# A banded attention and a gated feed-forward block on one core: the head of batch 0, the order of the loads and the last output tile are rewritten

## The chip, the core and the metric

The kernel runs on one core of a Trainium2 chip. The core has five engines with a queue of instructions each: TensorE (PE in the profile; its weight loads stand apart as PEld), VectorE (DVE), ScalarE (ACT), GpSimd (POOL) and SyncE (SP). Instructions of one engine run in the order in which they are written, and wait for other engines through semaphores. Transfers are issued from SP's, ACT's or GpSimd's queue. The metric is the device time of one execution in microseconds (us), lower is better. Before the change it is 253.46 us, the median of 9 runs (252.95 to 253.99).

## What is computed

There are four batches of 768 tokens with 8 heads of 64. Each token attends to the first 8 tokens and to the last 96, with a bias that falls with the distance; the result, with the heads side by side, goes through a gated feed-forward block.

```python
scores = q @ k.T / sqrt(64) - slope[h] * dist      # kept where key < 8 or 0 <= q - key < 96
a = exp(scores - max); a = a / (sum(a) + 1e-9)
x = (a @ v).transpose(0, 2, 1, 3).reshape(3072, 512)
g = x @ w_gate
out = (g / (1 + exp(-g)) * (x @ w_val)) @ w_out     # w_gate, w_val 512 x 1536, w_out 1536 x 512
```

Inputs and output are float32; the kernel computes with fp16 operands and float32 accumulation.

## The kernel before

**Tiles.** Heads go in four pairs (`hp` 0 to 3), two pairs make a quad (`g` 0, 1). Keys go in seven chunks of 120 (the last has 48), each with the 8 global keys in front, so that a chunk fills 128 rows: `kTs` holds the transposed keys in this form, `vSs[b]` the values. The first 8 rows of `vSs` are copied there by SP from `vG` (`copy_globals`). Queries of a batch are cut in two halves of 384 tokens, and a half is one token tile `t` of the feed-forward block (eight in all).

**Attention of a pair.** q and k are transposed on TensorE (L296, L270) or, for later pairs, by DMA (L399); scores go to a PSUM bank (L343, L366), ScalarE takes the exponential (L351, L375) into `at`, and a mask multiply puts the bias in (L355, L383, L386). In the first half of batch 0 there is no mask multiply: the bias is added by a matmul of `slopeI` and `dist` in front of the scores (L332). Values and denominators of a quad are matmuls with `vS` and with ones (L443); VectorE transposes and inverts the denominator (L453, L454, L459), and x is the product of the two (L499, L478).

**Feed-forward.** For a tile `t` and each of 12 blocks `f` of 128 columns: the gate's four matmuls and the value's four (L516), a tanh on ScalarE (L527), two multiplies on VectorE (L529, L533) into `hT`. Each 128-token row of the output is 12 matmuls with `wo` (L545), issued in four parts of three, one evacuation (L559) and one store by SP. Only the very last output row is evacuated in halves by ScalarE and VectorE, out of one bank, and stored by ACT's and SP's queues (L554 to L557).

**The head** is everything before the first product, for the first half of batch 0. q and k of pairs 0 and 1 come as float32 through SP and are cast by ScalarE and VectorE (`p_cast`, L589); those of pairs 2 and 3 are cast by the DMA, issued from GpSimd. V comes as one transfer of 384 KB (`v16`) in the row order that makes long packets, and TensorE brings it into chunks with twelve matmuls against permutation matrices (`p_perm`, L598), which VectorE builds; chunk 3 is cut at token 384 and has a tile of its own (`vCut`). `fill` issues matmuls on ones, with no use but to keep TensorE busy.

**Order.** It is written by hand. After the head, `stretches` pairs a run of feed-forward blocks with a list of attention steps; a step is put in whenever a quota has been earned by the blocks. Work on ScalarE and VectorE that may come later waits in the list `later`, of which one entry is taken with each group. `half1` is the second half of batch 0, `first(1)` the first half of batch 1, `both(b)` the second half of `b` and the first of `b + 1`. Loads are tied to blocks by `at_step`. GpSimd has no more than eight of its transfers under way: each issue waits for the one eight before it.

```python
stretches = [
    (ff(0, 0, 10), half1),
    (ff(0, 10, 12) + ff(1, 0, 3), []),
    (ff(1, 3, 12, (1, 1, 2)), fst),
    (ff(2, 0, 12, (1,)) + ff(3, 0, 12, (1,)), both(1)),
```

GpSimd's loads stand in this order: V, then k and q of pairs 2 and 3, `vG`, the weights of `f` 0 to 3 (`load_w(0, ·)`, four transfers of 256 KB), the second half of k and q of batch 0 (384 KB each), the weights of `f` 4 to 7 (`load_w(1, ·)`), the rest of V, the weights of `f` 8 to 11, `wo`, and batch 1.

Of the kernel before, what the change touches and what calls it, by code (L numbers as in the profile page):

```python
# [9 lines left out]
FP32 = mybir.dt.float32  # L10
# [6 lines left out]
WIN = 216  # L17
# [20 lines left out]
def kernel(  # L38
# [32 lines left out]
        np.concatenate([np.eye(128, 160, dtype=np.float16), dist_np], axis=1), name="consts")  # L71
# [25 lines left out]
    consts = sb.tile([128, 160 + 3 * WIN], FP16, name="consts")  # L97
    nc.sync.dma_start(out=consts, in_=const_dr.ap())
    identx, ident, dist = consts[:, 0:160], consts[:, 0:128], consts[:, 160:]
# [3 lines left out]
    q32 = sb2.tile([128, H // 2, J2 * D], FP32, name="q32", tag="qst")  # L103
    k32 = sb2.tile([128, H // 2, J2 * D], FP32, name="k32", tag="kst")
    q16 = sb2.tile([128, 2, H, J2 * D], FP16, name="q16", tag="qst")
    k16 = sb2.tile([128, 2, H, J2 * D], FP16, name="k16", tag="kst")
    v16 = sb.tile([128, H, J2 * D], FP16, name="v16")
    for hp in range(2):
        for st, src in ((k32, k), (q32, q)):
            nc.sync.dma_start(  # L110
                out=st[:, 2 * hp:2 * hp + 2, :],
                in_=src[0, 2 * hp:2 * hp + 2, 0:TB, :].rearrange(
                    "h (p j) d -> p h (j d)", p=128))

    def load_half(dst, src, half, h0, h1):
        nc.gpsimd.dma_start(
            out=dst, in_=src[0, h0:h1, TB * half:TB * half + TB, :].rearrange(
                "h (p j) d -> p h (j d)", p=128))

    vSs = [sb.tile([128, NCH, H, D], FP16, name=f"vS{b}") for b in range(B)]  # L120
    for b in range(1, B):
        nc.gpsimd.memset(vSs[b][:, 6, :, :], 0.0)
    load_half(v16, v, 0, 0, H)
    load_half(k16[:, 0, 4:8], k, 0, 4, 8)
    load_half(q16[:, 0, 4:8], q, 0, 4, 8)

# [4 lines left out]
    NC0 = 4  # L131
    perm = sb.tile([128, J2, NC0, 128], FP16, name="perm")
    nc.vector.memset(perm.rearrange("p j c m -> p (j c m)").bitcast(mybir.dt.uint32), 0)
    kTs = [sb.tile([128, NCH * 128], FP16, name=f"kT{i}") for i in range(NP)]

    vS3 = sb.tile([128, H, D], FP16, name="vCut")


    nc.vector.memset(vSs[0][:, 6, :, :], 0.0)
# [3 lines left out]
    for j in range(J2):  # L143
        nc.vector.tensor_copy(
            out=perm[:, j, :, NG + j::J2],
            in_=identx.rearrange("p (c m) -> p c m", c=NC0))
        n = (NG - j + J2 - 1) // J2
        nc.vector.tensor_copy(
            out=perm[:, j, :, j:NG:J2],
            in_=identx[:, 0:n].unsqueeze(1).broadcast_to([128, NC0, n]))  # L150

# [31 lines left out]
    def copy_globals(b):  # L183
        c0 = 3 if b == 0 else 0
        nc.sync.dma_start(
            out=vSs[b][0:NG, c0:, :, :],
            in_=vG[:, b, :, :].unsqueeze(1).broadcast_to([NG, NCH - c0, H, D]))
# [71 lines left out]
    class Pair:  # L259
# [30 lines left out]
        def transposes_half(self, half, tr, k_eng):  # L290
            hp = self.hp
            trq, trk = tr
            for st, dst in ((k16, trk), (q16, trq)):
                for j in range(J2):
                    for hi in range(2):
                        nc.tensor.transpose(  # L296
                            dst[64 * hi:64 * hi + 64, 128 * j:128 * j + 128],
                            st[:, half, 2 * hp + hi, D * j:D * j + D], ident)
# [28 lines left out]
        def bias(self, half, which):  # L327

            sc = banks("sc")
# [86 lines left out]
    class Quad:  # L416
# [19 lines left out]
        def weigh(self, half, dst, side):  # L436
            b, g = self.b, self.g
            parts = self.parts(half)
            for i, (c, cb, col, o, n) in enumerate(parts):
                vals = vS3 if (b, half, c) == (0, 0, 3) else vSs[b][:, c]  # L440
# [96 lines left out]
    def out_part(t, i, part):  # L537
# [10 lines left out]
        if part == 3:  # L548
            osb = sb2.tile([128, DM], FP32, name="osb", tag="osb")
            r0 = TB * t + 128 * i  # L550
            if t == NT - 1 and i == 2:

                oB = sb2.tile([128, DM // 2], FP32, name="osb", tag="th")
                nc.scalar.mul(out=osb[:, 0:DM // 2], in_=ops[:, 0:DM // 2], mul=0.5)  # L554
                nc.vector.tensor_scalar_mul(oB, ops[:, DM // 2:], 0.5)
                nc.scalar.dma_start(out=out[r0:r0 + 128, 0:DM // 2], in_=osb[:, 0:DM // 2])
                nc.sync.dma_start(out=out[r0:r0 + 128, DM // 2:], in_=oB)  # L557
            else:
                nc.scalar.mul(out=osb, in_=ops, mul=0.5)  # L559
                nc.sync.dma_start(out=out[r0:r0 + 128, :], in_=osb)  # L560

# [4 lines left out]
    load_globals()  # L566
    copy_globals(0)
# [9 lines left out]
    rings = {"t": ["x0", "x1"], "v": ["x2", "o0"]}  # L577

    def p_single(name, ring, dt=FP32):
        tags = rings[ring]  # L580
        tags.append(tags.pop(0))
        return single(name, tags[-1], dt)

    def p_bias(hp):
        pairs[0, hp].scs = [pairs[0, hp].bias(0, 0), pairs[0, hp].bias(0, 1)]

    def p_cast(hp, k_eng, q_eng):
        for eng, dst, src in ((k_eng, k16, k32), (q_eng, q16, q32)):
            eng(out=dst[:, 0, 2 * hp:2 * hp + 2], in_=src[:, 2 * hp:2 * hp + 2])  # L589

    def p_tr(hp, k_eng):
        tr = [p_single("trs", "t", FP16) for _ in range(2)]
        pairs[0, hp].transposes_half(0, [t[:, 0:TB] for t in tr], k_eng)

    def p_perm(c, eng):
        psv = p_single("psv", "v")
        for j in range(J2):
            nc.tensor.matmul(  # L598
# [237 lines left out]
```

The softmax here doesn't subtract the row's maximum and nothing guards it: scores larger than these inputs give would overflow.

## Time and profile before

| | |
|---|---|
| median of 9 runs | 253.46 us (252.95 to 253.99) |
| the profiled execution | 253.44 us, of which the span (first to last instruction) is 251.7 |
| granted TensorE clock | 0.998 |
| PE busy | 239.6 us (95%), 2384 matmuls |
| DVE busy | 166.9 us (66%) |
| ACT busy | 131.0 us (52%) |
| POOL busy | 106.2 us (42%), its DMA issues among it |
| GpSimd's DMA queue | 65408 packets, 13.83 MB, 67.4% of the 16 engines' span |
| one group of four matmuls, 128x384 | 0.65 us from start to start |

The page cuts the span into 40 slices of 6.29 us and gives the busy share of each in tenths. A timeline row is: start, duration (us), engine, line, operation, output and inputs, count, and in brackets how long the engine was idle before it and what ended that. The chain of work that ended last is given as start, duration, engine and line. A matmul's duration has its latency in it, so rows of TensorE overlap.

### The profile page before, as it was taken

The numbers are of one execution on the slowest core, as the hardware profiler recorded it, in microseconds if no ns is written. First come the engines' busy times: TensorE is split into PE (matmuls) and PEld (weight loads), VectorE is DVE, ScalarE is ACT, GpSimd is POOL, SyncE is SP. The second block draws the span as 40 slices with busy tenths as digits, with TensorE's granted clock in tenths as the row PEclk, the third lists the DMA queues.
The fourth block names the chain that finished last, engine by engine and source line by source line (L and its number), as shares of the span: only waits on it lengthen the run. The fifth ranks groups of instructions, "written<-read, shape, count | busy, mean of one in ns | idle before, by whom it ended". The sixth has DMA issues, their size and how long they took to land.

```text
span 251.7 us, 5999 instructions
## 1 busy us (share of the span) xinstructions
PE 239.6 (95%) x2384; PEld 135.3 (54%) x2384; DVE 166.9 (66%) x379; ACT 131.0 (52%) x290; POOL 106.2 (42%) x123
## 2 busy tenths in 40 slices
PE   7888999899889999999999999999999999999994
PEld 4564556464445555555555556555555555555541
DVE  6356779856785675979775656978766666556510
ACT  3475787559464565454753644555725634332221
POOL 9753674460056966904509776803030242200000
PEclk9999999999999999999999999999999999999999
DMA  6999999992850999996917998991011101100122
GB/s 160 176 205 179 180 203 207 173 134 52 126 69 8 160 131 110 188 139 110 81 44 83 147 154 97 144 101 43 0 44 42 44 0 44 43 26 19 42 83 83
DMA packets 86499, 25.63 MB, mean 102 GB/s; under 512 B 76288, under 2 KB 83528, under 8 KB 86472
## 3 DMA queue, kind: packets, MB, share of 16 engines
q0 software_dynamic: 65408, 13.83, 67.4%
q1 hardware_dynamic: 20920, 11.30, 22.4%
q8 instruction: 18, 0.29, 0.5%
q10 hardware_dynamic: 144, 0.13, 0.2%
q14 instruction: 9, 0.07, 0.1%
HBM read 28.63 MB, written 6.29 MB: 139 GB/s over the span
## 4 chain that ended last, share of the span: by engine, by line
PE 81%; DVE 8%; ACT 4%; DMA 3%; issue 1%; POOL 1%; DVEq 0%; ACTq 0%; POOLq 0%
PE ops L545 23%; PE gps L516 23%; PE vps L516 22%; DMA v<-in_v_dram 3%; PE sc L366 3%; PE num L443 3%; PE den L443 2%; DVE sl L529 2%; ACT at L351 2%; ACT th L527 1%; PE psv L598 1%; DVE hT L533 1%; PE trs L296 1%; PE sc L343 1%; DVE dT L453 1%
## 5 line engine op out<-in xcount | busy, mean ns | idle before, releaser
L529 DVE SCALAR_TENSOR_TENSOR sl<-th,gps 128x384 f32<-128x384 f32 x94 | 51.8, 551 | 45.4 <-ACT th L527 44.4
L527 ACT ACTIVATE th<-gps 128x384 f32<-128x384 f32 x94 | 46.5, 494 | 63.1 <-PE gps L516 61.6
L516 PE MATMUL gps<-xT,wg 128*128 128x384 f16 x376 | 77.0, 326 | 0.7 <-DVE xT L478 0.6
L516 PE MATMUL vps<-xT,wv 128*128 128x384 f16 x376 | 76.5, 326 | 0.5 <-DVE sl L529 0.4
L545 PE MATMUL ops<-wo,hT 128*128 128x512 f16 x288 | 75.5, 379 | 0.0
L533 DVE TENSOR_TENSOR hT<-vps,sl 128x384 f16<-128x384 f32 x94 | 51.7, 551 | 7.2
L478 POOL TENSOR_TENSOR xT<-ns,rb 128x384 f16<-128x384 f32 x24 | 24.2, 1028 | 75.4 <-DVE rb L459 61.3
L516 PEld LDWEIGHTS <-wg 128*128 128x128 f16 x384 | 35.8, 98 | 33.1 <-issue 3.1
L516 PEld LDWEIGHTS <-wv 128*128 128x128 f16 x384 | 36.8, 98 | 26.4 <-issue 2.1
L545 PEld LDWEIGHTS <-hT 128*128 128x128 f16 x288 | 27.4, 98 | 25.1 <-issue 0.4
L375 ACT ACTIVATE at<-sc 128x432 f16<-128x432 f32 x72 | 33.6, 535 | 9.0 <-PE sc L366 9.0
L171 POOL DMA_DIRECT2D vS<-in_v_dram x25 | 22.3, 898 | 9.6 <-DMA wg<-in_moe_w_gate_dram 2.5
L559 ACT ACTIVATE osb<-ops 128x512 f32<-128x512 f32 x23 | 13.7, 597 | 18.0 <-PE ops L545 18.0
L474 ACT COPY ns<-num 128x384 f32<-128x384 f32 x28 | 12.0, 482 | 12.0 <-PE num L443 11.2
L203 POOL DMA_DIRECT2D qst<-in_q_dram x20 | 16.8, 857 | 2.7 <-DMA wo<-in_moe_w_out_dram 1.6
L203 POOL DMA_DIRECT2D kst<-in_k_dram x20 | 17.0, 867 | 2.1 <-DMA wo<-in_moe_w_out_dram 1.0
L386 DVE TENSOR_TENSOR at<-at,masks 128x864 f16<-128x864 f16 x20 | 12.1, 605 | 4.6 <-ACT at L375 4.6
L351 ACT ACTIVATE at<-sc 128x432 f16<-128x432 f32 (+2 forms) x32 | 11.5, 447 | 3.9 <-PE sc L343 3.9
L386 POOL TENSOR_TENSOR at<-at,masks 128x864 f16<-128x864 f16 x4 | 7.3, 1822 | 13.6 <-ACT at L375 13.6
L443 PE MATMUL num<-at,vS 128*32 128x216 f16 (+6 forms) x560 | 12.0, 226 | 0.0
L443 PE MATMUL den<-at,ones 128*32 128x216 f16 (+6 forms) x288 | 9.2, 229 | 1.9 <-DVE at L383 1.4
L453 DVE STREAM_TRANSPOSE dT<-den 128x384 f32<-128x384 f32 x16 | 9.2, 576 | 1.8 <-PE den L443 1.7
(76 smaller groups left out, 169.9 us busy)
## 6 DMA issues: line engine op xcount, KB each, us to landing
out_dram<-osb SPq DMA_DIRECT2D x23, 256.0 KB, 2.0
vS<-in_v_dram POOLq DMA_DIRECT2D x21, 120.0 KB, 9.2
kst<-in_k_dram POOLq DMA_DIRECT2D x20, 96.0 KB, 5.1
qst<-in_q_dram POOLq DMA_DIRECT2D x20, 96.0 KB, 5.1
wg<-in_moe_w_gate_dram POOLq DMA_DIRECT2D x6, 256.0 KB, 9.0
wv<-in_moe_w_val_dram POOLq DMA_DIRECT2D x6, 256.0 KB, 9.5
wo<-in_moe_w_out_dram POOLq DMA_DIRECT2D x3, 512.0 KB, 11.0
k<-in_k_dram SPq DMA_DIRECT2D x2, 192.0 KB, 3.6
```

What stands on the lines that cost most here:

```text
L171: nc.gpsimd.dma_start(out=vSs[b][NG:NG + n, c, :, :], in_=v[b, :, KC * c:KC * c + n, :].rearrange("h p d -> p h d"))
L203: nc.gpsimd.dma_start(out=rows_of(st, b, h // 2)[:, :, h % 2, :], in_=src[b, h].rearrange("(t p) d -> p t d", p=128))
L351: nc.scalar.activation(out=at[:, hi, 0:col + n], in_=sc[hi][:, 0:col + n], func=AF.Exp, scale=scale)
L375: nc.scalar.activation(out=at[:, hi, :], in_=sc[hi][:, 0:BANK], func=AF.Exp, scale=scale)
L386: mul_eng.tensor_mul(at, at, m[:, :, o:o + BANK])
L443: nc.tensor.matmul(dst[r, o:o + n], lhsT=ones[:, 0:32] if side is None else vals[:, 4 * g + j, side::2], rhs=pairs[b, 2 * g + j // 2].at[c ...
L478: mul_eng.tensor_mul(self.x_out(half, side), srcs[side], self.rb)
L516: nc.tensor.matmul(gv[f, which][:, 0:TB], lhsT=w[:, c, 128 * f:128 * f + 128], rhs=x_of(t)[:, c, :], start=(c == 0), stop=(c == NC - 1))
L527: nc.scalar.activation(out=th, in_=dst[:, 0:TB], func=AF.Tanh, scale=0.5)
L529: nc.vector.scalar_tensor_tensor(out=sl, in0=th, scalar=1.0, in1=dst[:, 0:TB], op0=AluOp.add, op1=AluOp.mult)
L533: nc.vector.tensor_mul(hTs[t][:, f, :], dst[:, 0:TB], gv["sl"])
L545: nc.tensor.matmul(ops, lhsT=hTs[t][:, f, 128 * i:128 * i + 128], rhs=wo[:, f, :], start=(f == 0), stop=(f == NFF - 1))
```

## The change

- **Head.** One pair's q and k (pair 0) come as float32, k through SP and q through ACT's queue; pairs 1 to 3 are cast by the DMA, from GpSimd. V of batch 0 comes in chunks as for the other batches, with no permutation matmuls and no `vCut`; the four chunks of the first half stand ahead of the weights on GpSimd. The constants are split into `ident` (SP) and `dist` (ACT's queue). The memsets of `vSs` go from GpSimd to VectorE. Scores of a pair are two units of two banks, placed by name over the eight banks, and units of different pairs interleave with transposes.
- **Loads.** All of GpSimd's loads up to the end of batch 1 stand in one row after the first transposes. The weights of `f` 4 to 7 come ahead of the second half of k and q of batch 0.
- **Order.** The first five blocks have no attention steps, the ten steps of `half1` go into `f` 5 to 9. In `first(1)` the scores of pair 2 come ahead of the values of quad 0, and the DMA transposes of pairs 2 and 3 one step earlier. In `both` one spreading of keys goes one step earlier.
- **Last output row.** Two banks of 256 columns, 12 matmuls each; the first is evacuated by VectorE and stored by SP, the second by ScalarE and stored by its own queue.

```diff
-    identx, ident, dist = consts[:, 0:160], consts[:, 0:128], consts[:, 160:]
+    nc.sync.dma_start(out=ident, in_=const_dr.ap()[:, 0:128])
...
+    nc.sync.dma_start(out=k32, in_=half_of(k, 0, 0, 2))
+    nc.scalar.dma_start(out=q32, in_=half_of(q, 0, 0, 2))
+    nc.scalar.dma_start(out=dist, in_=const_dr.ap()[:, 128:])
...
-    for b in range(1, B):
-        nc.gpsimd.memset(vSs[b][:, 6, :, :], 0.0)
-    load_half(v16, v, 0, 0, H)
-    load_half(k16[:, 0, 4:8], k, 0, 4, 8)
-    load_half(q16[:, 0, 4:8], q, 0, 4, 8)
+    load_half(0, 2, 4)
+    load_half(0, 4, 8)
...
+    for b in range(B):
+        nc.vector.memset(vSs[b][:, 6, :, :], 0.0)
...
     def copy_globals(b):
-        c0 = 3 if b == 0 else 0
         nc.sync.dma_start(
-            out=vSs[b][0:NG, c0:, :, :],
-            in_=vG[:, b, :, :].unsqueeze(1).broadcast_to([NG, NCH - c0, H, D]))
+            out=vSs[b][0:NG],
+            in_=vG[:, b, :, :].unsqueeze(1).broadcast_to([NG, NCH, H, D]))
...
+    def out_last(t, i):
+        r0, n = TB * t + 128 * i, DM // 2
+        for side, (ev, dq) in enumerate(((nc.vector.tensor_scalar_mul, nc.sync),
+                                         (nc.scalar.mul, nc.scalar))):
+            ops = single("ops", f"a{i + side}")
+            c0 = n * side
+            for f in range(NFF):
+                nc.tensor.matmul(
+                    ops[:, 0:n], lhsT=hTs[t][:, f, 128 * i:128 * i + 128],
+                    rhs=wo[:, f, c0:c0 + n], start=(f == 0), stop=(f == NFF - 1))
+            osb = sb2.tile([128, n], FP32, name="osb", tag="th")
+            ev(osb, ops[:, 0:n], 0.5)
+            dq.dma_start(out=out[r0:r0 + 128, c0:c0 + n], in_=osb)
...
     load_globals()
+    for c in range(4):
+        load_v_rest(0, c)
     copy_globals(0)
...
+    def p_bias(hp, which, *tags):
+        pairs[0, hp].sc = pairs[0, hp].bias(0, which, [single("sc", t) for t in tags])
+
+    def p_sc(hp, which, *tags):
+        if tags:
+            p_bias(hp, which, *tags)
+        pairs[0, hp].scores_half(0, which, pairs[0, hp].sc)
+
+    def p_tr(hp, kt, qt, n_fill=0):
+        tr = [single("trs", t, FP16)[:, 0:TB] for t in (qt, kt)]
+        pairs[0, hp].transposes_half(0, tr, V, lambda: fill(n_fill))
...
+    fill(15)
...
+    p_tr(0, "x0", "x1", 2)
     load_w(0, 0)
     load_w(0, 1)
...
-    load_half(k16[:, 1], k, 1, 0, H)
-    load_half(q16[:, 1], q, 1, 0, H)
     load_w(1, 0)
     load_w(1, 1)
-    for c in range(3, NCH):
+    load_half(1, 0, H)
+    for c in range(4, NCH):
         load_v_rest(0, c)
+    load_w(2, 0)
+    load_w(2, 1)
     for b in range(1, B):
         copy_globals(b)
+    stage(1)
+    load_qk(1, 0, 4)
+    for g in range(3):
+        load_wo(g)
+    for hp in (2, 3):
+        for i in (1, 0):
+            for e in range(2):
+                load_rows(1, i, 2 * hp + e)
+    for c in range(NCH):
+        load_v_rest(1, c)
+    p_bias(0, 0, "a0", "a1")
+    p_sc(0, 0)
+    p_bias(0, 1, "a2", "a3")
+    p_tr(1, "x2", "o0")
+    p_sc(0, 1)
+    p_sc(1, 0, "x0", "x1")
+    p_tr(2, "a0", "a1")
+    p_sc(1, 1, "x2", "o0")
+    p_tr(3, "a2", "a3")
+    p_sc(2, 0, "a0", "a1")
+    quads[0, 0].denominators(single("den", "x0"))
+    p_sc(2, 1, "a2", "a3")
+    for side, tag in enumerate(("x1", "x2")):
+        quads[0, 0].numerators(side, single("num", tag))
+    p_sc(3, 0, "a0", "a1")
+    p_sc(3, 1, "a2", "a3")
...
     def first(b):
-        return [[tr(b, 0), tr(b, 1)],
-                [sc(b, 0, 0), sc(b, 0, 1)], [sc(b, 1, 0), sc(b, 1, 1), fetch(b, 2, 3)],
-                [sp(b, 2), va(b, 0, 0), sp(b, 3)],
-                [sc(b, 2, 0), sc(b, 2, 1)],
+        return [[tr(b, 0), tr(b, 1)], [sc(b, 0, 0), sc(b, 0, 1), fetch(b, 2, 3)],
+                [sc(b, 1, 0), sc(b, 1, 1), sp(b, 2)],
+                [sc(b, 2, 0), sc(b, 2, 1), sp(b, 3)], [va(b, 0, 0)],
                 [sc(b, 3, 0), sc(b, 3, 1)], [va(b, 1, 0)]]
...
-                [va(b, 0, 1)], [sp(n, 0), va(b, 1, 1), sp(n, 1)],
+                [va(b, 0, 1), sp(n, 0)], [va(b, 1, 1), sp(n, 1)],
...
-        (ff(0, 0, 10), half1),
+        (ff(0, 0, 5), []),
+        (ff(0, 5, 10), half1),
...
-    for i in range(3):
+    for i in range(2):
         for part in range(4):
             out_part(NT - 1, i, part)
+    out_last(NT - 1, 2)
```

## The prediction

> **What bounds the kernel now.** I read the page's slices first, then TensorE in order of time, then what lands when. Durations come from one profiled execution of 253.44 us: a span of 251.7 and 1.74 around it. The median of the runs shown is 253.46, so no correction is needed.
>
> ```profile
> PE   7888999899889999999999999999999999999994
> ...
> DMA  6999999992850999996917998991011101100122
> ```
>
> One slice is 6.29 us. TensorE (PE) is idle 12.1 us of 251.7 (busy 239.6). By windows, 4.9 of these lie before 22.8, 3.5 between 22.8 and 110, and 3.7 at the end. The DMA row is full from slice 2 to slice 9, to 57 us: in that stretch a load lands when the bytes ahead of it have passed, not when it is issued. The chain of the head, in order of time:
>
> ```profile
> 2.13 8.09 DMA v<-in_v_dram
> ...
> 10.26 1.46 PE psv L598 x6
> ...
> 21.73 1.03 DVE xT L499 x2
> ```
>
> V takes 8.09 us to land, PE permutes it, and the first products with both halves of x start at 22.34. What the loads do is read from GpSimd's timeline, where each issue waits for the eighth transfer before it, and from the DMA view of two windows (packets, MB), 35 to 40 and 25 to 30 us:
>
> ```profile
> 11.55 0.88 POOL L116 DMA_DIRECT2D q<-in_q_dram  x1
> ...
> 19.61 0.92 POOL L171 DMA_DIRECT2D vS<-in_v_dram  x1 [0.49 <-DMA wv<-in_moe_w_val_dram]
> ```
> ```profile
> q0 software_dynamic: 1023, 1.01, 122.7%
> ```
> ```profile
> q0 software_dynamic: 3500, 0.89, 177.1%
> ```
>
> The first full-size q load (second half of batch 0, heads 0 to 7) is issued at 11.55 and, at 12.9 us to landing, lands at 24.45. The second row says that the last of the first four weight loads landed by 19.6. The first window, all 1 KB packets, gives 5 us x 16 engines / 1023 = 78 ns per packet on an engine. The second (2974 packets under 512 B, nearly all of 128 B, and 526 of 1 KB) gives (80 - 526 x 0.078)/2974 = 13 ns for a small one.
>
> TensorE's timeline has the places where the loads and x are used:
>
> ```profile
> 26.17 0.33 PE L296 MATMUL trs<-consts,q 128*64 128x128 f16 x6
> ...
> 48.14 0.32 PE L516 MATMUL gps<-xT,wg 128*128 128x384 f16 x1 [0.61 <-DVE xT L478]
> ...
> 64.01 0.48 PE L443 MATMUL den<-at,ones 128*32 128x144 f16 x6 [0.71 <-DVE at L383]
> ```
> ```profile
> 248.04 0.38 ACT L554 ACTIVATE osb<-ops 128x256 f32<-128x256 f32 x1 [1.99 <-PE ops L545]
> ...
> 248.46 0.42 DVE L555 TENSOR_SCALAR osb<-ops 128x256 f32<-128x256 f32 x1 [7.79 <-ACT osb L554]
> 248.91 0.33 SPq L557 DMA_DIRECT2D out_dram<-osb  x1
> ```
>
> At 26.17 the second half of batch 0 starts, 1.7 after its q landed; at 48.14 the last piece of token tile 1's x arrives; at the end VectorE waits for ScalarE on the same PSUM bank.
>
> [...] SP's four small copies into vS, issued from 12.67, show 10 packets between 16 and 17 us and 49 in the next, so some 4 us behind GpSimd's queue. [...] So "casts by DMA" moves loads from SP's queue into the full one. [...]
>
> **The head.** Removed: 12 perm matmuls (2.9 us of PE), their four evacuations, the perm building on VectorE, 11 fills net (28 to 15 and 2), two of four SP/ACT k/q loads of 192 KB and their casts. Added: two 96 KB cast loads on GpSimd, four V chunks of 120 KB ahead of the weights, four V memsets (4 x 0.27, VectorE instead of 3 x 0.53 on GpSimd, which so issues 1.4 earlier). ScalarE's chain becomes the head's: four qT copies (0.48), eight 432-column exps and eight 168-column ones (1.36 a pair): 7.4 us of work, starting about 5.6, when q (now ahead on ACT's queue) has been cast and transposed. By hand along that order: exps of pair 0 to 7.4, qT of pair 1 and the rest of pair 0 to 8.4, first exps of pair 1 to 9.3; pair 2's q (9.2 by the bytes ahead of it) is copied by 10.1, pair 3's by 11.1, first exps of pair 2 to 12.2, and PE reaches the first numerator at about 12.2. Queued behind it are both score units of pair 3, and ScalarE waits for those. It needs V and the copied globals. vG landed at 5.51 + 7.1 = 12.6; ahead of it go 1024 packets of v (2.4 us at 38 ns, from 1691 small packets in 5 to 10 us) and 512 of SP (1.8 at 57 ns), and come 512 of k/q (1.2): 9.3 with the earlier start. SP then takes 0.9 to issue and some 4 to 5 to land: about 15.0. From first numerator to first product with both halves was 16.29 to 22.34, 6.05; ScalarE loses 0.8 of kT copies there: 5.3. So products start at 20.3 instead of 22.34: **2 us gained**, if the last first weights (19.6 + 0.1) are there, and they are.
>
> **The loads.** The order of the changed kernel has all of w(1) ahead of batch 0's second half of k and q. Ahead of q's landing: SP -1.8, v -2.4, k/q +1.2, four V chunks 4 x 960 x 13 ns / 16 = +3.1, w(1) 4 x 256 x 78 ns / 16 = +5.0: +5.1. The earlier start is worth 0.3, as the engines were already 70 to 93% busy with SP's loads. So q lands at 24.45 + 4.8 = **29.2** (27.3 to 31.5: 11 to 15 ns per small packet, and how far the slowest engine lags). Products f = 0 to 4 and the gate of 5 run without attention between: 20.3 + 2.25 to f = 2, + 6 x 0.65 + 0.65 = 27.1. w(1) lands at about 24.7 (29.7 before, less 4.8 for k/q, less 0.2), just in time. PE then stands before the q transposes for **2.1 us: the gain of the head is spent here**. Behind these transposes in PE's order stand the value of f = 5 and all of half 1; ScalarE and VectorE run dry with it.
>
> **Half 1, squeezed.** Ten attention steps now lie between f = 5 and 9 instead of 2 and 9. From the q transposes to the last x piece it took 26.17 to 48.14, 22.0; five product groups of 0.65 now come before, so 18.7 if nothing else changed. Per engine, by start to start: PE 13 x 0.65 + four scores x 0.74 + three transposes x 0.46 + two values x 1.03 = 15.0; ScalarE four exp quadruples x 1.39, 6 x 0.39 tanh, copies and masks = 13.1; VectorE 13 x 0.47, kT 4 x 0.6, masks 4 x 0.52, denominators and x = 14.9. All three are nearly full. Following the order by hand, PE waits 0.8 for kT of pair 2, 0.5 and 1.0 for masks in front of the two values, more for banks and ScalarE's order, and the last x piece comes 18.7 after the start too (17 to 20.5). 29.2 + 18.7 = 47.9 against 48.14: **-0.2**.
>
> **Batch 1 first half.** Loads in one row are hidden: the DMA engines are full until 57 either way with 0.2 MB less to move, and the first wo matmul (52.91) and pair 2's transposes by DMA come after. Those four transposes now precede the first output store on SP; they wait for rows that land by 57, and the store is due at 60.5, so neither holds the other. The new order puts the scores of pair 2 in front of values (0,0). Their keys are spread on VectorE behind the masks of pair 1, which end at 64.25; three copies later it is 64.85, and PE is there at 62.8. Then 0.5 scores, 1.95 products, 1.05 values, 2.65 products: the scores of pair 3 at 71.0 against 70.70: **+0.3** (-0.3 to +1). The wait at 64.01 goes, one of 2 us comes.
>
> **Both batches.** Spreading keys one step earlier lifts a copy off the tail after values (b,1,1), where PE waited 0.40 at 104.55: **-0.4** (-0.8 to 0).
>
> **Tail.** 24 matmuls of 256 columns for 12 of 512: 24 x 0.108 (fills, 10 in 1.27 less the first) = 12 x 0.216, nothing. VectorE's side is evacuated and sent during the second twelve; its serial 0.42 and the gap go: **-0.46** (-0.3 to -0.7).
>
> Sum: -0.2 + 0.3 - 0.4 - 0.46 = -0.76: a span of 250.9, **252.7 us**.
>
> **Rivals.**
> Slower, by one mechanism: q of the second half lands late. For: 128 B packets cost 14.7 ns in 50 to 55 us (5445 in 5 us), +0.4; weight loads lagged 3.5 us behind the sum of their packets, the later ones 2 to 3. At 31.2 it adds 2.0: 254.7. It decides from 30.0 on. Against: the difference method above takes the lag from the same load.
> Faster: loads are there when PE comes, at 27.1 or before; then 27.1 + 18.7 = 45.8 and 250.6. For: 5 to 10 us moved only 169 GB/s and 35 to 40 moved 204, so the new mix could do better. Against: 2.1 us are missing.
> The clock: PE stands 2.8 us before the first numerator and 2.1 before the q transposes, without the fills. If the clock halves, [...] the first case hides in the wait for q and the second falls on a stage where PE has 3.7 us of room: about +1, 253.7 to 254.
> Nothing moves: the pieces cancel to within 0.5; the change then does shorten the head, with nothing of it left at 48 us.
>
> **How the numbers follow.** As worked 0.42 (own range 251.7 to 253.3), late loads 0.30 (254.7), early loads 0.12 (250.6), clock 0.08 (253.9), cancelled 0.08 (253.4). 0.2% is 0.5 us, about what a measurement of this kernel can tell from no change. Faster 0.52, within it 0.10, slower 0.38: the near ends of the first case go to "same" and a few hundredths to "slower". Range 250.8 to 255.0.
>
> **What would show it.** Right: products of f = 0 complete near 20.3, PE's gap in front of the q transposes of about 2 us ending on the in_q load near 29, tile 1's last x piece near 48, a wait for VectorE's kT copies near 63, one evacuation at the end. Wrong: no gap there, or one over 3 us; numerators waiting past 17; a fill-like doubling of matmul times after a wait; half 1 over 20 us.

## The result, and the profile after

The changed kernel takes 254.88 us (median of 16 runs, 254.07 to 256.12) against 253.44 (53 runs, 252.06 to 256.52): a ratio of 1.0062, 95% interval 1.0046 to 1.0077. It is **slower by 0.6%**; the forecast was 252.7 and faster. Its profiled execution took 254.11 us with a span of 252.3, so it is one of the quicker ones, 0.77 under the median. A second profile (the first experiment) shows what that hides. Medians here are of all executions, ratios and intervals leave out the few slow ones (over 1.5% above the fastest of the same kernel); without them the 255.09 and 253.71 of two kernels below are 254.98 and 253.65.

The slices of the page, TensorE, its granted clock and the DMA share:

```profile
PE   7859988999789999999999999999999999999994
...
PEclk9968999999999999999999999999999999999999
...
DMA  8999999999810999991915998991011101101122
```

A new hole stands in slice 3 (12.6 to 18.9 us), with the granted clock down to 0.6 there and 0.8 in slice 4. The DMA row is full to slice 10 (63 us); before, it was full to slice 9, and the forecast had left that end at 57 us. TensorE's timeline says what the hole is (start, length, line, operation, and in brackets the idle time before it and what ended it):

```profile
15.35 1.20 PE L427 MATMUL num<-at,vS 128*32 128x216 f16 x32 [3.48 <-DMA vS<-vG]
...
21.82 0.79 PE L500 MATMUL gvps<-xT,wg 128*128 128x384 f16 x2
...
29.21 0.36 PE L280 MATMUL trs<-ident,q 128*64 128x128 f16 x6
...
49.02 0.81 PE L500 MATMUL vps<-xT,wv 128*128 128x384 f16 x4
...
65.42 0.55 PE L350 MATMUL sc<-qT,kT 64*128 64x216 f16 x8 [1.78 <-DVE kT L395]
...
105.61 0.81 PE L500 MATMUL vps<-xT,wv 128*128 128x384 f16 x4 [0.48 <-DVE sl L513]
```

The first numerators wait 3.48 us for SP's copies of the global rows. Products with both halves of x start at 21.82, hardly before the old 22.34. The kernel before has, of the same timeline,

```profile
22.34 0.79 PE L516 MATMUL gvps<-xT,wg 128*128 128x384 f16 x2 [0.93 <-DVE xT L499]
...
48.30 0.81 PE L516 MATMUL vps<-xT,wv 128*128 128x384 f16 x4
...
104.55 0.81 PE L516 MATMUL vps<-xT,wv 128*128 128x384 f16 x4 [0.40 <-DVE sl L529]
```

In the changed kernel the second half's q transposes start at 29.21 (before: 26.17). The first value product of token tile 1 starts at 49.02; before it was at 48.30, so here lies +0.72. By the scores of pair 3 (71.58, before 70.70) it is +0.88, by the product at 105.61 (before 104.55) +1.06. The end gives 0.48 back:

```profile
247.78 0.42 DVE L549 TENSOR_SCALAR osb<-ops 128x256 f32<-128x256 f32 x1 [6.05 <-PE ops L545]
...
249.09 0.38 ACT L549 ACTIVATE osb<-ops 128x256 f32<-128x256 f32 x1 [1.97 <-PE ops L545]
```

Only one half tile is left to evacuate after the last matmul. The chain of waits, in order of time, has in its head

```profile
16.09 13.08 DMA q<-in_q_dram
```

so the q load, issued at 16.09, landed at 29.17. TensorE had come to the k transposes in front of it at 28.75 and hardly waited.

### The profile page after: what moved, and what is told of

Read it like the earlier page. It is cut to its first block, busy times and chain, and to the rows that moved or that the text cites. A ratio compares the mean times of both kernels' runs of the same rounds, so it can differ in the third digit from the quotient of the medians.

```text
span 252.3 us, 5961 instructions
## 1 busy us (share of the span) xinstructions
PE 237.9 (94%) x2373; PEld 134.7 (53%) x2373; DVE 168.4 (67%) x373; ACT 129.5 (51%) x286; POOL 107.0 (42%) x124
## 4 chain that ended last, share of the span: by engine, by line
PE 71%; DVE 11%; DMA 8%; POOL 3%; ACT 3%; issue 2%; DVEq 0%; ACTq 0%; POOLq 0%
PE ops L529 21%; PE vps L500 20%; PE gps L500 20%; DMA q<-in_q_dram 5%; PE sc L350 3%; PE num L427 3%; DMA wv<-in_moe_w_val_dram 2%; DVE hT L517 2%; DVE sl L513 2%; PE den L427 2%; DVE kT L391 2%; DVE kT L394 1%; POOL vS L154 1%; PE ops L545 1%; ACT th L511 1%
## 5 line engine op out<-in xcount | busy, mean ns | idle before, releaser
L529 PE MATMUL ops<-wo,hT 128*128 128x512 f16 x276 | 72.9, 379 | 0.0
L529 PEld LDWEIGHTS <-hT 128*128 128x128 f16 x276 | 26.2, 98 | 23.7 <-issue 0.4
L154 POOL DMA_DIRECT2D vS<-in_v_dram x28 | 24.8, 893 | 2.9 <-DMA wg<-in_moe_w_gate_dram 2.1
L427 PE MATMUL num<-at,vS 128*32 128x216 f16 (+6 forms) x576 | 13.1, 235 | 3.5 <-DMA vS<-vG 3.5
L335 ACT ACTIVATE at<-sc 128x432 f16<-128x432 f32 (+2 forms) x32 | 11.8, 450 | 6.6 <-PE sc L327 6.6
L427 PEld LDWEIGHTS <-vS 128*32 128x32 f16 x576 | 11.0, 100 | 3.6 <-issue 3.6
L350 PE MATMUL sc<-qT,kT 64*128 64x216 f16 (+2 forms) x168 | 9.8, 241 | 1.8 <-DVE kT L395 1.8
```

The costliest lines, as they stand in the source:

```text
L154: nc.gpsimd.dma_start(out=vSs[b][NG:NG + n, c, :, :], in_=v[b, :, KC * c:KC * c + n, :].rearrange("h p d -> p h d"))
L350: nc.tensor.matmul(sc[hi][:, col:col + n], lhsT=self.kT[r, 128 * c:128 * c + 128], rhs=self.qT[r, q0:q0 + n], start=True, stop=True)
L427: nc.tensor.matmul(dst[r, o:o + n], lhsT=ones[:, 0:32] if side is None else vals[:, 4 * g + j, side::2], rhs=pairs[b, 2 * g + j // 2].at[c ...
L529: nc.tensor.matmul(ops, lhsT=hTs[t][:, f, 128 * i:128 * i + 128], rhs=wo[:, f, :], start=(f == 0), stop=(f == NFF - 1))
```

## The experiments

They ran in three sets; in these the kernel before has a median of 254.02 to 254.04, and each ratio is to that kernel in the same set. (The changed kernel's first comparison, in the second row, had 253.44.) The marks of their profiles, read from TensorE's timeline, in us ("+" is the changed kernel with that edit):

| kernel | products with both halves | q transposes, 2nd half | tile 1's first value | difference of the last two | median | ratio (95%) |
|---|---|---|---|---|---|---|
| before, first profile | 22.34 | 26.17 | 48.30 | 22.13 | 254.03 | 1 |
| changed, first profile | 21.82 | 29.21 | 49.02 | 19.81 | 254.88 | 1.0062 (1.0046-1.0077) |
| changed, again | 23.43 | 30.55 | 50.34 | 19.79 | 254.99 | 1.0048 (1.0029-1.0068) |
| + fills | 21.16 | 30.21 | 51.03 | 20.82 | 255.12 | 1.0051 (1.0025-1.0077) |
| + globals first | 20.43 | 30.12 | 51.08 | 20.96 | 255.11 | 1.0042 (1.0022-1.0062) |
| + globals first, order and spread undone | 20.26 | 24.42 | 47.95 | 23.53 | 253.26 | 0.9979 (0.9966-0.9993) |
| + globals first, half of w(1) | 22.32 | 29.44 | 49.21 | 19.77 | 253.83 | 0.9988 (0.9972-1.0004) |
| + half of w(1) | 22.59 | 29.72 | 49.49 | 19.77 | 255.09 | 1.0028 (1.0007-1.0049) |
| + globals first, order undone | 22.45 | 31.69 | 51.47 | 19.78 | 257.19 | 1.0142 (1.0105-1.0179) |
| + orders of batch 1 and both undone | 23.39 | 30.52 | 50.29 | 19.77 | 255.15 | 1.0050 (1.0030-1.0070) |
| before + tail | 21.99 | 25.82 | 47.95 | 22.13 | 253.71 | 0.9983 (0.9962-1.0004) |
| before + tail, split loads | 22.16 | 26.00 | 48.13 | 22.13 | 253.81 | 1.0006 (0.9982-1.0030) |
| split loads, spread, globals first, old orders | 21.56 | 25.40 | 47.53 | 22.13 | 252.21 | 0.9922 (0.9895-0.9950) |
| the same + fills | 21.18 | 25.01 | 47.15 | 22.14 | 252.76 | 0.9961 (0.9945-0.9976) |

A row is one execution, and a mark moves by more than 1 us between executions of one kernel; the medians decide.

### The changed kernel again

> The changed kernel, unchanged, for a second profile and to say how far it stands from the kernel before. Three theories are to be told apart in this set. Queue theory: the end is set by the landing of the second half of q and k of batch 0 at 29.2 us, with all ten attention steps squeezed between products f = 5 and 9 behind it; what happens before 29 us is free. Clock theory: the 3.5 us wait for the global rows of V in front of the first numerator halves TensorE's clock from 14 to 21 us, and that costs the end about 1 us. Order theory: the new order of batch 1 and of both batches' steps costs what the profile shows behind 48 us. All expect here 254.9 +/- 0.4, and the gap in front of the q transposes again under 0.5 us, q landing at 29.2 +/- 0.3.

No edit. 254.99 us. Its profiled execution took 255.44 (span 253.7), and here TensorE didn't come early:

```profile
17.02 1.20 PE L427 MATMUL num<-at,vS 128*32 128x216 f16 x32 [3.55 <-DMA vS<-vG]
...
30.55 0.33 PE L280 MATMUL trs<-ident,q 128*64 128x128 f16 x6
```

The numerators waited to 17.02, not 15.35. Of that delay of 1.7 us, 1.3 are left at the q transposes, and no gap stands in front of them. The q load was issued at 16.9 and took 13.1 us: it landed at 30.0, past the expected 29.2 +/- 0.3. So the head is late and q is late, and they arrive within 0.6 us of each other. Two things can set the start of half 1, and the next runs take them away one at a time.

### Clock kept: fills in the wait

```diff
+    warm = single("warm", "o0")
+    fill(28)
     for side, tag in enumerate(("x1", "x2")):
         quads[0, 0].numerators(side, single("num", tag))
```

> The changed kernel with 28 fill matmuls in front of the first numerators, which keep TensorE busy through the wait for the global rows of V, so the clock isn't halved. Clock theory: products with both halves of x start at about 20.6 instead of 21.8 and the time falls by 1, to 253.9 +/- 0.3. Queue theory: TensorE comes to the q transposes at about 27.7 and stands there until q lands at 29.2, so the gap grows from about 0.05 to 1.5 us and the time stays: 254.9 +/- 0.4.

255.12 us: no gain. The clock theory was right about the head and wrong about the end. TensorE's timeline of this run:

```profile
15.77 0.72 PE L427 MATMUL num<-at,vS 128*32 128x216 f16 x32 [0.93 <-DMA vS<-vG]
...
21.16 0.79 PE L500 MATMUL gvps<-xT,wg 128*128 128x384 f16 x2 [0.93 <-DVE xT L483]
...
30.21 0.36 PE L280 MATMUL trs<-ident,q 128*64 128x128 f16 x6 [1.73 <-DMA q<-in_q_dram]
```

From the first numerators to the products it now takes 21.16 - 15.77 = 5.39 us, against 6.47 and 6.41 in the two profiles without fills. The halved clock (in the first profile 0.50 was granted from 14.5 to 21 us) costs 1.0 to 1.1 us there. But TensorE then stands 1.73 us in front of q, and after that the clock is halved in half 1 instead (0.50 from 31.3 to 34.7 us), which takes 20.82 instead of 19.8.

### The wait taken away: global rows first

```diff
+    load_globals()
     load_half(0, 2, 4)
     load_half(0, 4, 8)
...
-    load_globals()
```

> The changed kernel with the global rows of V loaded first on GpSimd's queue, so that the wait of 3.5 us in front of the first numerators should be gone, with its clock loss. Clock theory: 3.5 us and the halved clock are gone, some of it reaches the end: 253.9 or less. Queue theory: first products with both halves at 18 to 19.5 us, TensorE at the q transposes at 25.5 to 27, a wait of 2 to 3.5 us there ending on the q load at 29.2 +/- 0.4, and the time unchanged, 254.9 +/- 0.4.

255.11 us, ratio 1.0042 against the changed kernel's 1.0048. The wait for the global rows is gone (two of 0.17 and 0.92 us for V's chunks are left) and products start at 20.43, but:

```profile
30.12 0.53 PE L281 MATMUL trs<-ident,q 128*64 128x128 f16 x6 [1.98 <-DMA q<-in_q_dram]
```

TensorE stands 1.98 us, as the forecast had it. Issued at 18.3 in this run, q took 11.8 us and lands at 30.1. Here too the clock is halved (0.50 from 29.9, just ahead of the wait's end, to 33.3 us), and half 1 takes 20.96. An earlier head alone buys nothing.

### Fewer bytes ahead of q, with and without the earlier head

```diff
         f0 = WF * n
+        WF1 = 256 if n == 1 else WF
...
-                out=w[:, 2 * g:2 * g + 2, f0:f0 + WF],
+                out=w[:, 2 * g:2 * g + 2, f0:f0 + WF1],
```

with the source cut likewise, and products f = 6 and 7 taking the columns of f = 4 and 5. First with the global rows in front:

> The changed kernel with the global rows of V first, and with the second weight load w(1) cut to 256 of its 512 columns, so that 0.5 MB less lies ahead of the second-half q; products f = 6 and 7 use the weights of f = 4 and 5, so the weights of 256 columns of gate and value are left out and the output isn't the reference's; TensorE's work is the same. Order of loads and squeeze of half 1 are those of the changed kernel. Queue theory (bytes ahead of q set it): q lands 2.5 us earlier than 30.1 (half of w(1)'s 5.0), the wait of 2.0 us in front of the q transposes and its clock loss go, and the time falls by 1.5 to 2.3 against the kernel with the globals first (255.1), to 252.8 to 253.6. Squeeze theory (what the steps between f = 5 and 9 lack is room on ScalarE and VectorE, whenever q lands): half 1 grows by what q gains, and the time stays over 254.5.

253.83 us: 1.28 under the kernel with the globals first alone. The low end of the expected gain was 1.5, so the size is a little under. The gain is read from the times: the intervals of the two ratios (1.0022 to 1.0062 and 0.9972 to 1.0004) don't meet. The one profile, of an execution of 254.30, doesn't show the earlier head: its numerators start at 14.29, but wait three times for V's chunks (0.30, 0.64 and 0.44 us), TensorE then runs slower (four score matmuls take 0.54 us at 17.81, and took 0.36 at 13.18), and products start at 22.32. What it shows is q, landed at 19.3 + 9.1 = 28.4, in front of TensorE, which came at 29.4 and didn't wait. Then without the globals in front:

> The changed kernel with w(1) cut to 256 of its 512 columns and nothing else (products f = 6 and 7 use the weights of f = 4 and 5, so 256 columns of gate and value weights are left out and the output isn't the reference's); the wait for the global rows of V stays. Two-bounds theory: the slow head (global rows at 15.4 to 17, then a halved clock) and the late q (30.1) bring TensorE to the q transposes at the same 29 to 30.5, each hides the other; q now lands at 27.6, but TensorE isn't there before 28.8 to 30.4, so the time falls by 0 to 0.5, to 254.5 to 255.0, while the two cures together gave 253.8. One-bound theory (late q alone): the time falls by 1.2 here too, to 253.8.

255.09 us. Here q landed at 16.7 + 10.3 = 27.0, yet TensorE wasn't there before 29.5, because the head was late:

```profile
16.18 1.20 PE L428 MATMUL num<-at,vS 128*32 128x216 f16 x32 [2.90 <-DMA vS<-vG]
...
29.72 0.33 PE L281 MATMUL trs<-ident,q 128*64 128x128 f16 x6
```

The changed kernel again: 254.99. Earlier q alone: 255.09. Earlier head alone: 255.11. Both: 253.83. That is what two bounds at the same time look like: each cure is hidden by what the other leaves in place. By ratios the first gains at most 0.2% (1.0028 against 1.0048, with intervals that overlap).

### Order of loads undone, without and with the spread

Both have the globals first and

```diff
+    load_half(1, 0, H)
     load_w(1, 0)
     load_w(1, 1)
-    load_half(1, 0, H)
```

In the first the ten steps stay between f = 5 and 9:

> The changed kernel with the global rows of V first and with the second half's k and q ahead of w(1) again, but with the ten steps still squeezed between f = 5 and 9: the order of loads undone without the spread. Theory of one front (the bytes ahead of 29 us are the same, and whichever load comes second lands at 28 to 30): w(1) lands at 28.3 and TensorE, with nothing but products to do, stands about 2.5 us in front of f = 4 and then starts half 1 at 29.5 to 30.3, so the time is that of the changed kernel, 255.0 +/- 0.5. Squeeze theory (only q's landing counts): half 1 starts as q has landed, at 27 or before, and the time is 253.3 or less.

257.19 us. The direction is that of the one front, the size was missed by 2.2 us. Timeline:

```profile
28.92 0.50 PE L501 MATMUL gps<-xT,wg 128*128 128x384 f16 x2 [1.02 <-DMA wg<-in_moe_w_gate_dram]
...
30.42 0.50 PE L501 MATMUL vps<-xT,wv 128*128 128x384 f16 x2 [0.67 <-DMA wv<-in_moe_w_val_dram]
...
31.69 0.33 PE L281 MATMUL trs<-ident,q 128*64 128x128 f16 x6
```

I had let all of w(1) land at 28.3. The gate columns did at about 28.9, the last value columns at 30.4, and q, long landed at 25.0, had to stand behind them: TensorE reaches its transposes at 31.69. In the second the steps are spread over f = 0 to 9 as in the kernel before:

```diff
-        (ff(0, 0, 5), []),
-        (ff(0, 5, 10), half1),
+        (ff(0, 0, 10), half1),
```

(with the weights and quota that go with it)

> The kernel of the run before with one thing undone: the second half of batch 0's k and q is loaded ahead of the second w(1) weight columns again, and its ten attention steps are spread over products f = 0 to 9 as in the kernel before. Queue theory: q lands near 24.4 us, the steps start near 24.5, the second columns land near 29.3 and the value product of f = 4 waits for them at most 1 us; the squeeze of half 1 is gone, so the last x piece comes at about 47.3 instead of 48.5 and the time is 253.6 +/- 0.6, 1.3 under the changed kernel. If instead half 1 doesn't matter (order theory: all that is lost is lost behind 48 us), the time is that of the run before.

253.26 us, ratio 0.9979: the loss is gone.

```profile
24.42 0.36 PE L281 MATMUL trs<-ident,q 128*64 128x128 f16 x6 [0.16 <-DMA q<-in_q_dram]
...
28.27 0.50 PE L501 MATMUL gps<-xT,wg 128*128 128x384 f16 x2 [1.20 <-DMA wg<-in_moe_w_gate_dram]
```

Attention steps fill the time until w(1) comes, and only 1.20 us of waiting are left. With the order alone undone it is 257.2, with order and spread 253.3: the interleaving of steps with products is what makes room for a load, and here the room was in front of w(1).

### The orders of batch 1 and of both batches

```diff
-        return [[tr(b, 0), tr(b, 1)], [sc(b, 0, 0), sc(b, 0, 1), fetch(b, 2, 3)],
-                [sc(b, 1, 0), sc(b, 1, 1), sp(b, 2)],
-                [sc(b, 2, 0), sc(b, 2, 1), sp(b, 3)], [va(b, 0, 0)],
+        return [[tr(b, 0), tr(b, 1)],
+                [sc(b, 0, 0), sc(b, 0, 1)], [sc(b, 1, 0), sc(b, 1, 1), fetch(b, 2, 3)],
+                [sp(b, 2), va(b, 0, 0), sp(b, 3)],
+                [sc(b, 2, 0), sc(b, 2, 1)],
...
-                [va(b, 0, 1), sp(n, 0)], [va(b, 1, 1), sp(n, 1)],
+                [va(b, 0, 1)], [sp(n, 0), va(b, 1, 1), sp(n, 1)],
```

> The changed kernel with the orders of batch 1's first half and of both batches' steps put back as in the kernel before; head, loads, squeeze and tail stay. Prediction's terms: +0.3 and -0.4 are undone, so the time would go up by 0.1, to 255.0. What the profiles read since: +0.2 and +0.1 are undone, so it falls by 0.3 (0 to 0.4), to 254.6; the wait of 1.8 us for VectorE's copies in front of pair 2's scores goes, waits of 0.7 for masks come back.

255.15 us, ratio 1.0050 against 1.0048: the timing can't tell either expectation. The trace can. From tile 1's first value to the same product of both batches it takes 106.50 - 50.29 = 56.21 us, against 105.61 - 49.02 = 56.59 and, in the second profile, 106.92 - 50.34 = 56.58 with the new orders. Eight profiles with the new orders, whatever their head, took 56.58 to 56.62, the three of the rebuilt kernel with the old ones 56.21 or 56.22: the new orders cost 0.4. (The kernel before took 56.25 in its first profile, and 56.96 and 57.04 in the two below.)

### The tail alone, on the kernel before

The kernel before, with the last output tile made in two banks by the changed kernel's function:

```diff
-    for i in range(3):
+    for i in range(2):
         for part in range(4):
             out_part(NT - 1, i, part)
+    out_last(NT - 1, 2)
```

> The kernel before with the new last output tile alone. Prediction's term for the tail: -0.46 (-0.3 to -0.7), so 0.2% faster than before, ratio 0.9982. Rival: the last store's landing sets the end whichever queue it is on, and the gain is under 0.2. From the last matmul's end to the span's end 3.25 instead of 3.73 us is expected.

Ratio 0.9983 (0.9962 to 1.0004), at the expected 0.9982. The interval takes in no change, so the time alone doesn't prove it, but the trace has the same end as the changed kernel, with the span's end 3.2 us after ScalarE's start in both:

```profile
247.07 0.42 DVE L565 TENSOR_SCALAR osb<-ops 128x256 f32<-128x256 f32 x1 [6.05 <-PE ops L561]
...
248.38 0.38 ACT L565 ACTIVATE osb<-ops 128x256 f32<-128x256 f32 x1 [1.97 <-PE ops L561]
```

### What the new head is worth: split loads

The changed kernel with the globals first, the steps spread, the old orders of batch 1 and both batches, and

```diff
+    load_half(1, 0, 4)
     load_w(1, 0)
     load_w(1, 1)
-    load_half(1, 0, H)
+    load_half(1, 4, 8)
```

> The changed kernel with the global rows of V first; the second half's k and q of heads 0 to 3 ahead of w(1) and of heads 4 to 7 behind it; the ten steps of half 1 spread over f = 0 to 9; and the orders of batch 1 and of both batches as in the kernel before. Queue theory: q of heads 0 to 3 lands by 23, w(1) by 27.5 instead of 28.3, so that the wait of 1.2 us for w(1) seen with only the order restored shrinks to under 0.5, heads 4 to 7 land by 29.5 and are used from 30.5; the time is 252.0 (251.4 to 252.8), 0.6 to 0.8% under the kernel before. If another engine bounds the stretch from 24 to 48, the wait comes back elsewhere in it and the time stays near 253.1.

252.21 us, **ratio 0.9922 (0.9895 to 0.9950): it beats both kernels**. The timeline has no wait for q or w(1) in half 1:

```profile
25.40 0.33 PE L281 MATMUL trs<-ident,q 128*64 128x128 f16 x6
...
30.52 0.33 PE L281 MATMUL trs<-ident,q 128*64 128x128 f16 x6
```

Heads 0 to 3 are used at 25.40. Heads 4 to 7, issued at 20.8 and 9.1 us on their way, land at 29.9 and are used at 30.52. The same split on the kernel before (with the new tail, so that what differs is the head with its global rows, and the row of batch 1's loads):

> The kernel before with the new last tile and with its second half's k and q split: heads 0 to 3 ahead of w(1), heads 4 to 7 behind it. Says what the new head is worth when the loads no longer stand in its way. In the kernel before w(1) is there as the value of f = 4 needs it, and TensorE comes to the q transposes no sooner, so nothing is gained: 253.7 +/- 0.4, as with the new tail alone, and the new head with the same split (252.2) is then worth 1.5. If the head is worth nothing, this kernel runs at 252.2 as well.

253.81 us against 253.71 with the tail alone: the split gives the old head nothing. Against the rebuilt kernel with the split it is 1.6 slower, but not all of that is the head. The last piece of tile 1's x, first in the rebuilt kernel, then in the one before with the split:

```profile
47.36 0.32 PE L501 MATMUL gps<-xT,wg 128*128 128x384 f16 x1 [0.61 <-DVE xT L463]
```
```profile
47.97 0.32 PE L516 MATMUL gps<-xT,wg 128*128 128x384 f16 x1 [0.61 <-DVE xT L478]
```

So 0.6 of the difference is there by then, out of 1.4 between the two spans (250.4 and 251.8). The other 0.8 comes up in batch 1, between 67 and 75 us: in the kernel before with the split, VectorE's first two copies of pair 3's keys stand on the chain of waits with 0.99 and 0.88 us, in the rebuilt one they aren't among the chain's longest pieces (0.75 us and more), and TensorE waited up to 1.1 instead of 0.7 us for masks. The profile with the tail alone loses 0.74 in the same place against the first profile of the kernel before, which has no such loss. The profiles give the rebuilt head 0.6; whether the 0.8 comes from the row of loads or varies from execution to execution is not shown.

Last, the clock once more, where no late q hides it: `fill(20)` before the first numerators of the split kernel.

> The fastest kernel so far (globals first, k and q split, steps spread, orders of batch 1 as before) with 20 fill matmuls in front of the first numerators. Its profile showed TensorE's clock halved from 15 to 21.6 us after gaps of 1.2 and 0.4 us, with products at 20.3. Clock theory: with the clock kept, products start at 19 or before and up to 1 us reaches the end: 251.2. Loads theory: the second weights land at 27 to 27.5 and heads 4 to 7 at 29.8 whatever the clock, so at most 0.4 is gained: 251.8 to 252.4; where the wait isn't there, the fills cost up to 0.5.

252.76 us, ratio 0.9961 (0.9945 to 0.9976), not under 252.21. Its profile has the full clock (1.0 over the span, against 0.986) and tile 1's first value at 47.15 instead of 47.53. The clock theory's gain of 1 isn't there; whether the fills cost 0.5, as the times say, or gain 0.4, as the two profiles say, stays open.

## Why the prediction was wrong

**What bounds the kernel.** Right: in these runs q landed when the bytes ahead of it had passed. With 0.5 MB of w(1) taken from there it came at 28.4 instead of 30.1 (globals first) and at 27.0 instead of 29.2 to 30.0. What was not drawn from it is that both kernels end their head on the same front. Before, w(1) lands at 29.7, as f = 4 needs its last columns; after, q lands at 29.2 to 30.1. The bytes ahead are about the same (0.2 MB less, by the forecast), and so is most of TensorE's work up to there.

**The head.** This step failed. It forecast numerators at 15.0 and products 5.3 us later, at 20.3. Numerators came at 15.35, 16.18, 16.93 and 17.02 in the four profiles with the changed kernel's head, and products 6.4 to 6.5 after them, at 21.8 to 23.4: instead of 2 us gained, from 0.5 gained to 1.1 lost. The 5.3 was right for a full clock (5.39 with fills). The clock rival named the place, where 1.0 to 1.1 us were lost, and let the wait for q hide it, which the fills bear out. Its +1 was an estimate of mine that no trace of before shows. The price in the head belonged into the main sum of the head all the same. By itself this step cost the end little: in the first profile q landed at 29.17, as forecast, and TensorE was there; in the second it came 0.55 after q; and with the head alone mended the time stayed. Mended together with the late q it was worth 1.3 us (253.83).

**The loads.** The mechanism was right, the size was off at the late end: q at 29.2 in the first profile, but at 29.9 to 30.1 in the next four with all of w(1) ahead (issue plus time to landing). The rival of the late load was said to decide from 30.0 on; the median of 254.88 lies close to its 254.7, but by luck. The 254.7 needed q at 31.2, 2.0 late. Landing at 30.0 accounts for 0.8 of the 2.2 us by which the forecast was missed; half 1 (0.95 over the forecast) and both batches (0.6) come to about the rest. The wait of 2.1 us was right only where the head was mended (1.73 and 1.98).

**Half 1, squeezed.** The second failing step. From the q transposes to tile 1's first value, 18.7 plus the gate matmul's 0.16 were forecast. Six profiles with the squeeze took 19.77 to 19.81 where TensorE hadn't stood right before it, and two took 20.8 and 21.0 where it had and the clock was halved. Spread, it is 22.13 or 22.14 in five kernels, 23.53 with a wait for w(1). So the squeezed half must start by 48.30 - 19.8 = 28.5 us to break even, and it started at 29.2 or later in every profile that has it.

The waits that the forecast named were right. They are longer than the idle times in the brackets (0.72 and 0.71), because matmuls of a step also start late one by one. From start to start, the score step at 34.15 takes 1.70 us where one without a wait takes 0.73, and the two value steps take 1.44 and 2.04 where 1.03 was put down: 0.97, 0.41 and 1.01, against 0.8, 0.5 and 1.0. The values of quad 1, before and after, each with the mask multiply that they need:

```profile
42.48 0.72 PE L443 MATMUL den<-at,ones 128*32 128x72 f16 x18
...
43.76 0.82 PE L516 MATMUL gps<-xT,wg 128*128 128x384 f16 x4
```
```profile
42.19 0.61 DVE L355 TENSOR_TENSOR at<-at,masks 128x864 f16<-128x864 f16 x1
```
```profile
42.41 0.42 PE L427 MATMUL den<-at,ones 128*32 128x72 f16 x10
43.54 0.34 PE L427 MATMUL den<-at,ones 128*32 128x216 f16 x8 [0.71 <-DVE at L339]
...
44.45 0.82 PE L500 MATMUL vps<-xT,wv 128*128 128x384 f16 x4
```
```profile
42.89 0.59 DVE L339 TENSOR_TENSOR at<-at,masks 128x864 f16<-128x864 f16 x1
```

The mis-sized term is "more for banks and ScalarE's order". TensorE's own work adds to 14.85, not 15.0, so 18.7 - 14.85 - 2.3 left 1.55 for it, and it was 19.65 - 14.85 - 2.4 = 2.4 (19.65 is 19.81 less the 0.16). Part of it stands at the end: the last products before tile 1's first value start 0.74, 0.94 and 0.93 us apart instead of 0.65. VectorE's timeline there:

```profile
47.48 0.55 DVE L517 TENSOR_TENSOR hT<-vps,sl 128x384 f16<-128x384 f32 x1
47.95 0.55 DVE L462 TENSOR_TENSOR xT<-ns,rb 128x384 f16<-128x384 f32 x1
48.42 0.55 DVE L513 SCALAR_TENSOR_TENSOR sl<-th,gps 128x384 f32<-128x384 f32 x1
```

hT ends at 48.03 and a gate product starts at 48.09; sl ends at 48.97 and the value product starts at 49.02. So the backlog of VectorE seems to hold the products' banks; this is read from the times, and no run tried it. It isn't new: in the kernel before the same starts lie 0.74, 0.93 and 1.56 apart, the last with a wait of 0.61 for x. Against that kernel (22.13 less five groups of 0.65, 18.88) the squeeze takes 0.93 more: 1.17 more in the two value steps, 0.3 each in the second score step and in a product at 32.11, and 0.6 less at this end.

**Batch 1 first half.** Forecast +0.3. The scores of pair 3 come 71.58 - 49.02 = 22.56 us after tile 1's first value, before 70.70 - 48.30 = 22.40: +0.16, with the expected wait of 1.8 for the copies in place of one for masks.

**Both batches.** Failed, by a small sum. Forecast -0.4; from the scores of pair 3 to the product at 105.61 it is 34.03, before 33.85: +0.18. The wait that was to go is still there, 0.48 instead of 0.40. The second spreading of keys starts 0.7 us earlier ahead of that product, but its first copy takes longer. Before and after:

```profile
102.47 0.59 DVE L407 COPY kT<-kN 128x720 f16<-128x720 f16 x1
102.98 0.98 DVE L410 COPY kT<-kN 128x48 f16<-128x48 f16 x1
```
```profile
102.80 1.33 DVE L391 COPY kT<-kN 128x720 f16<-128x720 f16 x1
104.05 0.98 DVE L394 COPY kT<-kN 128x48 f16<-128x48 f16 x1
```

The longer copy pushes sl back by what the move had won.

**Tail.** Right: -0.48 for -0.46.

**The sum** for the first profile: +0.72 + 0.16 + 0.18 - 0.48 = +0.58, and the spans differ by 0.6. For the second it is 2.04 + 0.18 + 0.15 - 0.48 = +1.89, and the spans differ by 2.0. The median lies between. Of the forecast's -0.76, the -0.2 at tile 1 was missed by 0.9 to 2.2 and the -0.4 of both batches by 0.6.

## What to carry to other kernels

Where two things reach a point within a microsecond of each other, here a late head and a late load, neither cure alone shows in the time (255.11 and 255.09 us against 254.99, both together 253.83); find both before judging either. The load order was worth nothing here without the work order: with the order of loads alone undone, q landed at 25.0 and was used at 31.69, behind the products that waited for w(1), and the kernel took 257.19 us; with the steps spread as well it took 253.26. A load that is needed in parts can be issued in parts, around the load that competes with it: in the rebuilt kernel that took the stretch from the q transposes to tile 1's first value from 23.53 to 22.13 us, in the kernel before, where no load was late, it brought nothing.

## What the hardware showed

The forecast's "fill-like doubling" is this: in the kernel before, the first 12 fills (from 1.20) took 2.74 us and ten later ones (from 6.12) 1.27: 0.23 against 0.13 each, with a granted clock of 1.00 in both places.

TensorE's granted clock fell to 0.50 with gaps of different length: with one of 3.48 us in the changed kernel (from 14.4 on), with one of 1.98 in the run with the globals first, with one of 1.73 in the run with fills. The windows of the last (TensorE's busy time is the first figure after the length, the granted clock follows POOL's bracket), around its one gap of 1.73 us from 28.48 to 30.21:

```profile
30.00:31.00 1.00, 0.79 (x9) 0.51 (x10) 0.00 (x0) 0.39 (x1) 0.30 (x1) 1.00 1.54 194
...
32.00:33.00 1.00, 1.00 (x7) 0.46 (x5) 0.52 (x3) 0.85 (x3) 1.00 (x3) 0.50 1.24 207
...
35.00:36.00 1.00, 1.00 (x16) 0.53 (x15) 0.14 (x1) 0.89 (x3) 0.98 (x2) 1.00 1.29 203
```

The clock halves at about 31.3, when TensorE has been working again for 1.1 us, and is back at 34.7. With the gap of 1.98, which ended at 30.12, it was halved from 29.9 to 33.3. A single gap of 1.20 in the kernel with order and spread undone left it full (1.00 in each us from 26 to 32). But in the split kernel gaps of 1.24 and 0.41 us, in front of 14.90 and 15.57, were enough:

```profile
14.50:15.00 0.50, 0.10 (x4) 0.10 (x4) 0.00 (x0) 0.00 (x0) 0.00 (x0) 0.99 1.28 204
15.00:15.50 0.50, 0.17 (x4) 0.00 (x1) 0.00 (x0) 0.00 (x0) 0.36 (x1) 0.50 1.28 229
```

Two gaps of 1.02 and 0.67, in front of 28.92 and 30.42 with the order alone undone, show no slower matmuls after them (six q transposes take 0.33 us at 31.69, and took 0.53 at 30.12 under the halved clock of the run with the globals first). So in these runs the length of one gap doesn't decide; what does is not shown. The clock stayed halved for 3.4 us in the runs with fills and with the globals first, and for 6.8 us in the heads of the changed kernel (14.4 to 21.2, first profile) and of the split one (15.0 to 21.8).

VectorE's copy of 48 columns took 0.17 us in one place and 0.98 in another. The profiles of the kernel before and of the changed kernel (the first one) have 20 such copies. Nine took 0.97 or 0.98, and each lay beside a GpSimd multiply (in the changed kernel the copy at 104.05 beside the two multiplies from 103.93 to 105.96). Eleven took 0.17: nine had no GpSimd multiply beside them, two (68.80 and 157.82 in the kernel before) started together with one all the same. No run took the multiply away. In the stretch of both batches the move of the first spreading of keys brought it beside such a multiply (97.48 to 99.55): its copies took 0.98 and 0.97 us from 97.70 on, and 0.34 and 0.17 before (from 98.39).
